# Writing out the order of all five queues in an attention loop, with decays per chunk and four more constant matmuls

## The chip, the cores and the metric

The kernel runs on one core of a Trainium2 chip. The metric is the time on the device in microseconds (us), the median of several executions. The profiled execution has a time of its own, and inside it a span from its first to its last instruction. The engines are PE (TensorE: matrix products into PSUM), DVE (VectorE), ACT (ScalarE), POOL (GpSimd) and SP (SyncE, which here only issues DMAs). Each takes its instructions from one queue, in order.

## The reference, cut to what matters

```python
B, H, S, D = 4, 8, 576, 64
gamma = 1 - 2.0 ** (-5 - arange(H))
Dmat = where(i >= j, gamma[h] ** (i - j), 0)
ret = ((q @ k.T) / sqrt(D) * Dmat) @ v          # retention, no softmax
x = ret.transpose(0, 2, 1, 3).reshape(B * S, H * D)
x = (silu(x @ w_gate) * (x @ w_val)) @ w_out    # 512 -> 1536 -> 512
y = relu(x @ w2_in) ** 2 @ w2_out               # 512 -> 2048 -> 512
```

The weights w_* are int64 words that hold doubles' bits; the kernel turns them into fp32 pairs (a high and a low part) on the chip.

## The kernel before, in words

**Attention.** The loop runs over n = 0 to 17 and handles 16 pairs of heads, each pair 128 partitions wide. The sequence of 576 is cut into four chunks of 128 and one of 64. For pair n, `scores(n, 0..3)` makes q k products within each of the four chunks (PE, tile `s`, into PSUM), and DVE multiplies by the mask of decays to `p_sb` (L439). `scores(n, (4,))` does the same for the last, short chunk; its result is `pl`. `states(n)` makes K V of each of four chunks (tile `kvs`) and sums them up over the chunks into `sb` (ACT copies the first, DVE adds three, L459). Two iterations later `apply(n, False)` and `apply(n, True)` sum q times state and p times v for the four chunks and for the last one, and ACT evicts to `xy` (L488). The bank that `apply(n - 2, True)` writes to is the one in which `scores(n, (4,))` left its result, so it waits until DVE has read that into `pl`. `prep_state` scales k (tile `kv_sb`, L410, on DVE for the first four pairs, then on POOL) and q (tile `qs`, L414, POOL) by decays that belong to absolute positions, for all chunks: `kscale` has a column for each chunk, `qscale` has 448.

**Loads.** `load(n)` issues on SP qk and kv of pair n, 576 KB each, for the first four pairs also mask and qscale. qk has three buffers, kv four.

**Weights.** A unit is 128 x 512 words. It goes through five steps, `pump` by `pump`: step 1 two ACT instructions (L161, L162) on the raw load; step 2 DVE L164; step 3 ACT and DVE split the unit before into its high and low part (L145, L146 `w_lo`), then DVE L168; step 4 L170; step 5 L179. `fill` is 1 from iteration 3 on. There are two raw buffers. In the loop 14 units are converted.

**Early projection.** Iterations 6 to 17 each do twelve matmuls of the first feed-forward layer for its first 512 tokens (`hidden1_early`), alternately for `g` and `v`, on x split into a high (ACT, `xh`) and a low part (DVE, `xl`).

**What sets the order.** A planner orders each engine's instructions from costs that it assumes, and keeps what the data demand. In the loop PE alone is held to the order of the code: `matmul` puts each instruction behind the one before it. DVE, ACT, POOL and SP are as planned. Behind the loop (`chain["on"] = False`) all is planned.

PE's fp32 matmul appears as two rows in the trace. Matmul rows all have line 98, so they are told apart by tile.

Of the kernel before, what the change touches and what calls it, by code (L numbers as in the profile page):

```python
# [18 lines left out]
NP = H // 2  # L19
# [21 lines left out]
WA = 20  # L41
# [14 lines left out]
def retention_moe_kernel(  # L56
# [34 lines left out]
    chain = {"on": False, "last": None}  # L91

    def matmul(*args, **kw):

        with ExitStack() as behind:
            if chain["on"] and chain["last"] is not None:
                behind.enter_context(tc.issue_after(chain["last"]))
            m = nc.tensor.matmul(*args, **kw)  # L98
        if chain["on"]:
            chain["last"] = m.ins  # L100
        return m
# [10 lines left out]
    def prefetch(upto):  # L112

        while loads["next"] <= min(upto, len(order) - 1):
# [13 lines left out]
            nc.sync.dma_start(out=raw, in_=src.rearrange("p (a n) -> p a n", a=2))  # L128
# [13 lines left out]
    def parts_unit(i):  # L142
        wf = w_t.pop(i).bitcast(F32)
        hi, lo = weight_tiles()
        nc.scalar.copy(hi, wf)  # L145
        nc.vector.tensor_tensor(out=lo, in0=wf, in1=f32(hi), op=ALU.subtract)  # L146
        units[order[i]] = (hi, lo)

    def conversion():
        ts = nc.vector.tensor_scalar  # L150
        for i in range(len(order)):
# [9 lines left out]
            nc.scalar.activation(out=low, in_=low16, func=AF.Copy, scale=2.0**-13)  # L161
            nc.scalar.activation(out=wf, in_=high.bitcast(F32), func=AF.Abs)  # L162
# [7 lines left out]
            nc.vector.scalar_tensor_tensor(  # L170
# [7 lines left out]
            for to, lo in adds:  # L178
                nc.vector.tensor_tensor(out=to, in0=to, in1=lo, op=ALU.add)  # L179
# [35 lines left out]
    def split_x(ph, n, cc):  # L215
# [9 lines left out]
        nc.scalar.copy(hi, src)  # L225
        nc.vector.tensor_tensor(out=lo, in0=src, in1=f32(hi), op=ALU.subtract)
        xs[ph, n, cc] = (hi, lo)

    def three(dst, a, b, first, last):
        (ah, al), (bh, bl) = a, b  # L230
        matmul(dst, ah, bh, start=first, stop=False)
        matmul(dst, ah, bl, start=False, stop=False)
        matmul(dst, al, bh, start=False, stop=last)
# [23 lines left out]
    def halves(key, t, early=False):  # L257
# [6 lines left out]
        nc.scalar.copy(hi, t)  # L264
        nc.vector.tensor_tensor(out=lo, in0=t, in1=f32(hi), op=ALU.subtract)  # L265
        hs[key] = (hi, lo)

    def hidden1(n, f, then=None):
# [3 lines left out]
        nc.scalar.activation(out=t, in_=g, func=AF.Sigmoid)  # L272
        yield
        nc.vector.tensor_tensor(out=t, in0=g, in1=t, op=ALU.mult)  # L274
        yield
        nc.vector.tensor_tensor(out=t, in0=vv, in1=t, op=ALU.mult)  # L276
# [5 lines left out]
    def hidden1_early(k):  # L282

        f, what = k // 2, "gv"[k % 2]
        if k == 0:
            for cc in range(CC):
                split_x(1, 0, cc)
        (ps,) = project(1, 0, f, (what, what))
        if what == "g":
            early_t[f] = t = t_p.tile([P, 512], F32, tag="t", name="t")  # L290
            nc.scalar.activation(out=t, in_=ps, func=AF.Sigmoid)
        t = early_t[f]
        nc.vector.tensor_tensor(out=t, in0=ps, in1=t, op=ALU.mult)
        if what == "v":
            halves((1, 0, f), early_t.pop(f), early=True)
        if k == 2 * HALF - 1:
            for cc in range(CC):
                split_x(1, 1, cc)

    def hidden2(n, f):  # L300
# [3 lines left out]
        nc.scalar.activation(out=t, in_=ps, func=AF.Relu)  # L304
        yield
        nc.vector.scalar_tensor_tensor(  # L306
# [10 lines left out]
    def out1(n, f):  # L317
# [14 lines left out]
        for cc, a in enumerate(acc.pop((1, n))):  # L332
# [5 lines left out]
            if n == 0 and f0:  # L338
                nc.vector.tensor_tensor(out=dst, in0=a[:, :m], in1=dst, op=ALU.add)
            elif cc % 2:  # L340
                nc.vector.tensor_copy(dst, a[:, :m])
            else:
                nc.scalar.copy(dst, a[:, :m])
            if n == 0 and f0 == 0:
                nc.sync.dma_start(out=part[:, cc, :], in_=dst)

    def out2(n, f):
# [7 lines left out]
        if f == F2 - 1:  # L355
            for tt, a in enumerate(acc.pop((2, n))):
# [3 lines left out]
                if tt % 2:  # L360
                    nc.vector.tensor_copy(t, a)
                else:
                    nc.scalar.copy(t, a)
                r0 = CHUNKS[2][n][0] + tt * P
                nc.sync.dma_start(out=out[r0:r0 + P, :], in_=t)
# [4 lines left out]
    with ExitStack() as st:  # L370
# [13 lines left out]
        def warm():  # L384

            one = const.tile([P, 256], F32, tag="one", name="one")
            nc.vector.memset(one, 1.0)
            ps = bank("g")
            for _ in range(WARM):
                matmul(ps[:, :256], one[:, :P], one, start=True, stop=True)  # L390

        def load(n):
# [234 lines left out]
```

## Time and profile before

| what | value |
|---|---|
| median of three runs | 953.1 us (951.22, 953.1, 954.19) |
| profiled execution, time | 950.97 us |
| its span | 949.2 us |
| PE busy in the span | 923.5 us (97%) |
| DVE, ACT, POOL busy | 469.0, 328.1, 33.7 us |
| mean granted clock | 0.986 |

The span is 1.77 us shorter than the time of the same execution. A busy share is a mean over stages: the attention loop ends at about 137.7 us, and the two layers fill the rest.

### The profile page before, as it was taken

The page shows a single profiled execution, that of the slowest core. Times are in us where ns is not written, and L with a number is a line of the kernel's source. Part 1 is how long each engine was busy: PE and PEld are TensorE (multiplying, and loading weights), DVE is VectorE, ACT ScalarE, POOL GpSimd, SP SyncE. Part 2 cuts the span into 40 slices and gives each one's busy share as a digit, 9 for nine tenths or more (in the row PEclk, how much of TensorE's full clock was granted, in tenths as well). Part 3 has the DMA queues.
Part 4 walks back from the last instruction along what each step waited for, and adds up shares of the span by engine and source line. Part 5 has one row for each costly group of instructions (what it writes and reads, how often), then busy time and mean ns, then how long its engine had stood idle before and what let it go on. Part 6 is the DMA issues. An engine that isn't in the chain of part 4 may idle for free.

```text
span 949.2 us, 12499 instructions
## 1 busy us (share of the span) xinstructions
PE 923.5 (97%) x5144; PEld 771.5 (81%) x5144; DVE 469.0 (49%) x849; ACT 328.1 (35%) x597; POOL 33.7 (4%) x35
## 2 busy tenths in 40 slices
PE   8499999999999999999999999999999999999998
PEld 6377778788888998888888888888888888888897
DVE  3858667798423332223799888233224222322232
ACT  1443444564312121112566565232223222322232
POOL 2133300000000000000000000000000000000000
PEclk7799999999999999999999999999999999999999
DMA  8756524442100000000244321001001000100010
GB/s 336 248 186 208 197 89 136 137 150 95 60 1 1 2 1 1 1 1 25 69 132 143 122 89 44 1 1 45 1 1 44 1 1 1 45 0 1 1 45 23
DMA packets 22025, 63.60 MB, mean 67 GB/s; under 512 B 2256, under 2 KB 3792, under 8 KB 21968
## 3 DMA queue, kind: packets, MB, share of 16 engines
q1 hardware_dynamic: 21968, 62.81, 19.8%
q8 instruction: 40, 0.66, 0.3%
q14 instruction: 17, 0.14, 0.0%
HBM read 57.03 MB, written 5.77 MB: 66 GB/s over the span
## 4 chain that ended last, share of the span: by engine, by line
PE 81%; DMA 8%; DVE 7%; ACT 2%; issue 1%; SPq 1%; ACTq 0%; DVEq 0%
PE a L98 34%; PE v L98 23%; PE g L98 23%; DMA raw<-in_w 6%; DVE w L170 1%; DVE w L179 1%; DVE w_lo L146 1%; DMA qk_sb<-in_qk 1%; DVE w L164 1%; DMA part<-part_sb 1%; ACT raw L161 1%; DVE p_sb L439 1%; DVE w L168 1%; DVE w_lo L265 0%; ACT w L162 0%
## 5 line engine op out<-in xcount | busy, mean ns | idle before, releaser
L265 DVE TENSOR_TENSOR h_lo<-t,h_hi 128x512 fp32r<-128x512 f32 (+1 forms) x134 | 85.1, 635 | 67.1 <-ACT h_hi L264 66.7
L264 ACT CAST h_hi<-t 128x512 fp32r<-128x512 f32 (+1 forms) x134 | 77.2, 576 | 118.1 <-DVE t L276 64.5
L98 PE MATMUL g<-xh,w_hi 128*128 128x512 f32 (+1 forms) x304 | 114.1, 375 | 0.8 <-ACT xh L225 0.8
L98 PE MATMUL v<-xh,w_hi 128*128 128x512 f32 (+1 forms) x304 | 113.7, 375 | 0.0
L98 PE MATMUL g<-xh,w_lo 128*128 128x512 f32 (+1 forms) x304 | 113.3, 373 | 0.0
L98 PE MATMUL g<-xl,w_hi 128*128 128x512 f32 (+1 forms) x304 | 113.2, 372 | 0.0
L98 PE MATMUL v<-xh,w_lo 128*128 128x512 f32 (+1 forms) x304 | 113.2, 372 | 0.0
L98 PE MATMUL v<-xl,w_hi 128*128 128x512 f32 (+1 forms) x304 | 113.2, 372 | 0.0
L98 PE MATMUL a<-w_lo,h_hi 128*128 128x512 f32 x288 | 112.3, 390 | 0.0
L98 PE MATMUL a<-w_hi,h_hi 128*128 128x512 f32 x288 | 112.2, 390 | 0.0
L98 PE MATMUL a<-w_hi,h_lo 128*128 128x512 f32 x288 | 109.8, 389 | 0.0
L98 PE MATMUL a<-h_lo,w_hi 128*128 128x512 f32 (+1 forms) x216 | 78.9, 366 | 0.0
L98 PE MATMUL a<-h_hi,w_lo 128*128 128x512 f32 (+1 forms) x216 | 78.9, 365 | 0.0
L98 PE MATMUL a<-h_hi,w_hi 128*128 128x512 f32 (+1 forms) x216 | 77.0, 366 | 1.2 <-ACT h_hi L264 1.2
L306 DVE SCALAR_TENSOR_TENSOR t<-g,t 128x512 f32<-128x512 f32 (+1 forms) x40 | 25.5, 637 | 105.5 <-ACT t L304 105.4
L274 DVE TENSOR_TENSOR t<-g,t 128x512 f32<-128x512 f32 (+1 forms) x54 | 34.0, 630 | 85.1 <-ACT t L272 84.8
L306 DVE SCALAR_TENSOR_TENSOR t<-v,t 128x512 f32<-128x512 f32 (+1 forms) x40 | 25.5, 638 | 92.4 <-ACT t L304 92.1
L98 PEld LDWEIGHTS g<-xh,w_hi 128*128 128x128 f32 x304 | 57.2, 188 | 11.5 <-ACT xh L225 1.2
L98 PEld LDWEIGHTS v<-xh,w_hi 128*128 128x128 f32 x304 | 57.3, 188 | 10.3 <-issue 0.2
L98 PEld LDWEIGHTS g<-xh,w_lo 128*128 128x128 f32 x304 | 57.3, 188 | 10.1
L98 PEld LDWEIGHTS v<-xh,w_lo 128*128 128x128 f32 x304 | 57.3, 188 | 10.1
L98 PEld LDWEIGHTS g<-xl,w_hi 128*128 128x128 f32 x304 | 57.3, 188 | 9.8
(88 smaller groups left out, 1486.0 us busy)
## 6 DMA issues: line engine op xcount, KB each, us to landing
raw<-in_w SPq DMA_DIRECT2D x51, 512.0 KB, 3.6
kv_sb<-in_kv SPq DMA_DIRECT2D x16, 576.0 KB, 5.0
xy<-in_w SPq DMA_DIRECT2D x17, 512.0 KB, 3.8
qk_sb<-in_qk SPq DMA_DIRECT2D x15, 576.0 KB, 5.0
out<-o_sb SPq DMA_DIRECT2D x18, 256.0 KB, 2.3
part<-part_sb SPq DMA_DIRECT2D x4, 256.0 KB, 2.8
xy<-part SPq DMA_DIRECT2D x1, 1024.0 KB, 5.3
qs_sb<-in_qscale SPq DMA_DIRECT2D x4, 224.0 KB, 7.4
```

Source lines behind the costliest of these rows:

```text
L98: m = nc.tensor.matmul(*args, **kw)
L146: nc.vector.tensor_tensor(out=lo, in0=wf, in1=f32(hi), op=ALU.subtract)
L161: nc.scalar.activation(out=low, in_=low16, func=AF.Copy, scale=2.0**-13)
L164: ts(out=wf, in0=wf, scalar1=TINY, scalar2=HUGE, op0=ALU.max, op1=ALU.min)
L168: ts(out=w, in0=w, scalar1=3, scalar2=0x3FFFFFFF, op0=ALU.logical_shift_left, op1=ALU.bitwise_and)
L170: nc.vector.scalar_tensor_tensor(out=w, in0=high, scalar=0xC0000000, in1=w, op0=ALU.bitwise_and, op1=ALU.bitwise_or)
L179: nc.vector.tensor_tensor(out=to, in0=to, in1=lo, op=ALU.add)
L264: nc.scalar.copy(hi, t)
L265: nc.vector.tensor_tensor(out=lo, in0=t, in1=f32(hi), op=ALU.subtract)
L274: nc.vector.tensor_tensor(out=t, in0=g, in1=t, op=ALU.mult)
L306: nc.vector.scalar_tensor_tensor(out=t, in0=ps, scalar=0.0, in1=t, op0=ALU.max, op1=ALU.mult)
L439: nc.vector.tensor_tensor(out=pt[:w], in0=ps[:w, :, :nx * w].rearrange("p h (c q) -> p h c q", c=nx), in1=mask_sb[:w, hp, :, None, :w].to_ ...
```

## The change

Every engine gets a chain of its own (`Chained`): within the loop each instruction is put behind the one before it on the same engine. The code's order is then the order of the five queues, so parts of the loop are moved: the load of kv for pair n + 1 comes ahead of that of qk for n + 2, `prep_state(n + 1)` goes to the end of the iteration, `apply(n - 2, True)` behind the early projection, the splits of x for the projection to one in each of the iterations 3 to 6, those for the next 512 tokens behind the loop. The pumps stand at other places: five steps an iteration as before, four in iteration 3.

Decays belong to chunks: k is scaled by one column of `kscale` for all chunks (two ACT multiplies of 128x256), q by 128 columns that repeat (two POOL instructions of 384 and 64 columns), and the sum of states multiplies the state so far by gamma to the 128 (scalar_tensor_tensor). Of `qscale` 161 columns are loaded instead of 448. In the first pair two matmuls on the constant tile stand behind its scores and two behind its K V (`warm(2)`). WA goes from 20 to 21, so 15 units are converted in the loop.

The diff, cut; `nc.tensor`, `nc.vector`, `nc.scalar`, `nc.gpsimd`, `nc.sync` become `pe`, `dve`, `act`, `pool_e`, `sp` everywhere:

```diff
-WA = 20
+WA = 21
...
+    class Chained:
+        def __init__(self, engine):
+            self.engine, self.last = engine, None
+        def __getattr__(self, name):
+            op = getattr(self.engine, name)
+            def traced(*args, **kw):
+                with ExitStack() as behind:
+                    if chain["on"] and self.last is not None:
+                        behind.enter_context(tc.issue_after(self.last))
+                    i = op(*args, **kw)
+                if chain["on"]:
+                    self.last = i.ins
+                return i
+            return traced
+    pe, dve, act, pool_e, sp = map(Chained, (nc.tensor, nc.vector, nc.scalar, nc.gpsimd, nc.sync))
...
     def hidden1_early(k):
         f, what = k // 2, "gv"[k % 2]
-        if k == 0:
-            for cc in range(CC):
-                split_x(1, 0, cc)
...
-        if k == 2 * HALF - 1:
-            for cc in range(CC):
-                split_x(1, 1, cc)
...
+        def load_qk(n):
             b, hp = pairs[n]
             qk_t[n] = qk_p.tile([P, 2, S], F32, tag="qk", name="qk_sb")
+            for at in (slice(0, CUT), slice(CUT, S)) if n == 0 else (slice(0, S),):
+                sp.dma_start(out=qk_t[n][:, :, at], in_=qk[b, hp][:, :, at])
+                if n == 0 and at.start == 0:
+                    sp.dma_start(out=ks_sb, in_=kscale)
+        def load_kv(n):
+            b, hp = pairs[n]
             kv_t[n] = kv_p.tile([P, 2 * NC - 1, P], F32, tag="kv", name="kv_sb")
+            sp.dma_start(out=kv_t[n], in_=kv[b, hp])
             if n < NP:
-                dma(out=mask_sb[:, n], in_=mask[:, n])
-                dma(out=qs_sb[:, n], in_=qscale[:, n])
+                sp.dma_start(out=mask_sb[:, n], in_=mask[:, n])
+                sp.dma_start(out=qs_sb[:, n], in_=qscale[:, n, P:P + qs_sb.shape[-1]])
...
-            kn = kv_t[n][:, NC:, :].rearrange("p t (h d) -> p t h d", h=2)
-            (nc.gpsimd if n >= NP else nc.vector).tensor_tensor(
-                out=kn, in0=kn, in1=ks_sb[:, hp].to_broadcast([P, NC - 1, 2, D]), op=ALU.mult
-            )
+            for h, r in enumerate(rs):
+                kn = kv_t[n][:, NC:, r]
+                act.mul(kn, kn, ks_sb[:, hp, 1, h])
             qs = q_p.tile([P, S - P], F32, tag="qs", name="qs")
-            nc.gpsimd.tensor_tensor(
-                out=qs, in0=qk_t[n][:, 0, P:], in1=qs_sb[:, hp, :], op=ALU.mult
-            )
+            for c, m in ((0, 3 * P), (3 * P, D)):
+                w = min(m, P)
+                pool_e.tensor_tensor(
+                    out=qs[:, c:c + m].rearrange("p (c q) -> p c q", q=w),
+                    in0=qk_t[n][:, 0, P + c:P + c + m].rearrange("p (c q) -> p c q", q=w),
+                    in1=qs_sb[:, hp, None, :w].to_broadcast([P, m // w, w]), op=ALU.mult,
+                )
...
-                nc.vector.tensor_tensor(out=sb[:, c], in0=ps[:, c], in1=sb[:, c - 1], op=ALU.add)
+                dve.scalar_tensor_tensor(
+                    out=sb[:, c], in0=sb[:, c - 1], scalar=qs_sb[:, pairs[n][1], -1:], in1=ps[:, c],
+                    op0=ALU.mult, op1=ALU.add,
+                )
...
-        load(0)
-        load(1)
+        load_qk(0)
+        load_kv(0)
+        load_qk(1)
         prep_state(0)
...
+            if nxt:
+                load_kv(n + 1)
             if n + 2 <= last:
-                load(n + 2)
+                load_qk(n + 2)
             if n == FROM - 3:
                 prefetch(1)
-            if nxt:
-                prep_state(n + 1)
             if new:
                 scores(n, range(NC - 1))
-            pump(fill)
+            if n == 0:
+                warm(2)
+            pump(fill if n == FROM - 3 else 2 * fill)
             if old:
                 apply(n - LAG, False)
             pump(fill)
+            if LAG < n <= LAG + CC:
+                split_x(1, 0, n - LAG - 1)
             if new:
                 scores(n, (NC - 1,))
+            pump(fill)
+            if new:
                 states(n)
+            if n == 0:
+                warm(2)
             pump(fill)
             if FROM <= n < FROM + 2 * HALF:
                 hidden1_early(n - FROM)
-            pump(fill)
             if old:
                 apply(n - LAG, True)
-            pump(fill)
-
+            if nxt:
+                prep_state(n + 1)
+        for cc in range(CC):
+            split_x(1, 1, cc)
     chain["on"] = False
```

## Rows read from the trace of the kernel before

**Rows 1.** The page: granted TensorE clock (tenths of full speed) in 40 slices of the span.

```profile
PEclk7799999999999999999999999999999999999999
```

**Rows 2.** Busy time in three stretches; then PEclk, DMA share, GB/s.

```profile
0.00:10.00 10.00, 6.44 (x44) 4.62 (x44) 2.68 (x6) 1.50 (x2) 1.24 (x8) 0.93 0.71 228
10.00:25.00 15.00, 13.13 (x156) 10.99 (x156) 7.98 (x17) 4.00 (x9) 4.07 (x4) 0.71 1.03 414
...
51.00:137.70 86.70, 83.88 (x941) 65.88 (x937) 60.14 (x118) 35.49 (x78) 22.87 (x19) 1.00 0.51 171
```

**Rows 3.** PE's timeline: start, duration, instructions merged, idle before and its releaser.

```profile
1.19 3.78 PE L98 MATMUL g<-one 128*128 128x256 f32 x8 [1.19 <-DVE one L387]
...
20.82 1.16 PE L98 MATMUL s<-qk_sb 64*128 64x128 f32 x16
...
31.32 0.48 PE L98 MATMUL s<-qs,sb 64*64 64x64 f32 x4 [5.21 <-DVE pl L439]
...
32.14 2.08 PE L98 MATMUL s<-qk_sb 64*128 64x128 f32 x16
...
43.40 0.48 PE L98 MATMUL s<-qs,sb 64*64 64x64 f32 x4 [5.04 <-DVE pl L439]
...
51.00 1.16 PE L98 MATMUL s<-qk_sb 64*128 64x128 f32 x16
...
58.93 1.16 PE L98 MATMUL s<-qk_sb 64*128 64x128 f32 x16
...
66.20 1.16 PE L98 MATMUL s<-qk_sb 64*128 64x128 f32 x16
...
140.07 0.50 PE L98 MATMUL g<-xh,w_hi 128*128 128x512 f32 x1 [0.78 <-ACT xh L225]
```

**Rows 4.** Timelines of DVE (31 to 33 us) and of POOL (at 32 us).

```profile
30.99 0.28 DVE L439 TENSOR_TENSOR pl<-s,mask_sb 64x128 f32<-64x128 f32 x1
...
31.96 1.41 DVE L168 TENSOR_SCALAR w<-w 128x512 uint32<-128x512 uint32 x1
...
31.95 1.14 POOL L414 TENSOR_TENSOR qs<-qk_sb,qs_sb 128x448 f32<-128x448 f32 x1 [3.06 <-issue]
```

**Rows 5.** The chain that ended last, first 60 us: start, length, what.

```profile
14.43 7.89 DMA raw<-in_w
...
52.76 1.90 PE o L98 x28
...
55.53 2.94 PE g L98 x12
```

**Rows 6.** Tile kv_sb, to 130 us: its loads.

```profile
DMA to landing us min/median/max: 3.6/5.0/8.4
```

**Rows 7.** Groups of instructions by shape, to 160 us: busy us, mean ns, idle before.

```profile
L439 DVE TENSOR_TENSOR p_sb<-s,mask_sb 128x1024 f32<-128x1024 f32 x16 | 19.4, 1215 | 0.5 <-PE s L98 0.3
...
L170 DVE SCALAR_TENSOR_TENSOR w<-raw,w 128x512 uint32<-128x512 uint32 x19 | 14.6, 767 | 0.1
L179 DVE CUSTOM_DVE_ANT_0 w<-raw,w 128x1024 uint16<-128x1024 uint16 x19 | 14.5, 765 | 0.1
...
L146 DVE TENSOR_TENSOR w_lo<-w,w_hi 128x512 fp32r<-128x512 f32 x19 | 13.1, 690 | 1.4 <-ACT w_hi L145 1.4
...
L459 DVE TENSOR_TENSOR sb<-kvs,sb 128x64 f32<-128x64 f32 x48 | 10.5, 218 | 10.2 <-ACT sb L457 9.6
...
L168 DVE TENSOR_SCALAR w<-w 128x512 uint32<-128x512 uint32 x20 | 9.3, 467 | 0.2
L488 ACT COPY xy<-o 128x512 f32<-128x512 f32 x16 | 9.2, 576 | 9.7 <-PE o L98 9.6
...
L226 DVE TENSOR_TENSOR xl<-xy,xh 128x512 fp32r<-128x512 f32 x8 | 6.1, 770 | 6.3 <-ACT xh L225 6.2
...
L488 ACT COPY xy<-s 128x64 f32<-128x64 f32 x16 | 3.3, 209 | 3.3 <-PE s L98 3.3
```

**Rows 8.** Line 164, to 51 us: duration min/median/max, first and last start.

```profile
L164 DVE TENSOR_SCALAR w<-w x6: 414/422/430, 23.6 to 43.3; 128x512 f32<-128x512 f32 x6
```

More of the change, by code (lines that the diff above doesn't have):

```diff
@@ L89, in f32 @@
         return ap.bitcast(F32)
[L91 to L101, printed above, removed]
+    chain = {"on": False}
+    class Chained:
[13 more added lines that the diff above has]
+    pe, dve, act, pool_e, sp = map(Chained, (nc.tensor, nc.vector, nc.scalar, nc.gpsimd, nc.sync))
     units = {}
@@ L160, in conversion @@
             wf = w.bitcast(F32)
-            nc.scalar.activation(out=low, in_=low16, func=AF.Copy, scale=2.0**-13)
-            nc.scalar.activation(out=wf, in_=high.bitcast(F32), func=AF.Abs)
+            act.activation(out=low, in_=low16, func=AF.Copy, scale=2.0**-13)
+            act.activation(out=wf, in_=high.bitcast(F32), func=AF.Abs)
             yield
@@ L178, in conversion @@
             for to, lo in adds:
-                nc.vector.tensor_tensor(out=to, in0=to, in1=lo, op=ALU.add)
+                dve.tensor_tensor(out=to, in0=to, in1=lo, op=ALU.add)
             del raw_t[i]
@@ L224, in split_x @@
             lo = xs_p.tile([P, N], F32R, tag="xl", name="xl")[:, :m]
[L225 to L226 removed]
+        act.copy(hi, src)
+        dve.tensor_tensor(out=lo, in0=src, in1=f32(hi), op=ALU.subtract)
         xs[ph, n, cc] = (hi, lo)
@@ L230, in three @@
         (ah, al), (bh, bl) = a, b
-        matmul(dst, ah, bh, start=first, stop=False)
-        matmul(dst, ah, bl, start=False, stop=False)
-        matmul(dst, al, bh, start=False, stop=last)
+        pe.matmul(dst, ah, bh, start=first, stop=False)
+        pe.matmul(dst, ah, bl, start=False, stop=False)
+        pe.matmul(dst, al, bh, start=False, stop=last)
     def cut(pair, a, n):
@@ L263, in halves @@
             lo = h_p.tile([P, N], F32R, tag="hl", name="h_lo")[:, :m]
-        nc.scalar.copy(hi, t)
-        nc.vector.tensor_tensor(out=lo, in0=t, in1=f32(hi), op=ALU.subtract)
+        act.copy(hi, t)
+        dve.tensor_tensor(out=lo, in0=t, in1=f32(hi), op=ALU.subtract)
         hs[key] = (hi, lo)
@@ L338, in out1 @@
             if n == 0 and f0:
-                nc.vector.tensor_tensor(out=dst, in0=a[:, :m], in1=dst, op=ALU.add)
+                dve.tensor_tensor(out=dst, in0=a[:, :m], in1=dst, op=ALU.add)
             elif cc % 2:
-                nc.vector.tensor_copy(dst, a[:, :m])
+                dve.tensor_copy(dst, a[:, :m])
             else:
-                nc.scalar.copy(dst, a[:, :m])
+                act.copy(dst, a[:, :m])
             if n == 0 and f0 == 0:
-                nc.sync.dma_start(out=part[:, cc, :], in_=dst)
+                sp.dma_start(out=part[:, cc, :], in_=dst)
     def out2(n, f):
@@ L382, in retention_moe_kernel, with warm @@
         pairs = [(b, hp) for b in range(B) for hp in range(NP)]
-        def warm():
-            one = const.tile([P, 256], F32, tag="one", name="one")
-            nc.vector.memset(one, 1.0)
+        def warm(k):
             ps = bank("g")
-            for _ in range(WARM):
-                matmul(ps[:, :256], one[:, :P], one, start=True, stop=True)
-        def load(n):
+            for _ in range(k):
+                pe.matmul(ps[:, :256], one[:, :P], one, start=True, stop=True)
+        def load_qk(n):
```

61 lines of the change are left out of this document (28 added, 33 removed).

## The prediction, made before the changed kernel was run

> **What bounds the kernel now.** I read the page first, for the clock by slice [rows 1], then the stretches [rows 2], then TensorE's (PE's) timeline of the first 140 us [rows 3], because only code up to the end of the attention loop is changed. What can be won lies in the first 137.7 us, where the loop's last product ends. The reader is to see three things there.
>
> First, from 51.00 us on, an iteration with its early projection costs 7.27 us (58.93 to 66.20), and the stretch 51.0 to 137.7 has 2.82 us of PE idle in 86.70 [rows 2, 3]. That stretch is nearly full.
>
> Second, ahead of 51.0 it is not. The scores of iteration 3 start at 20.82 us, those of iteration 4 at 32.14, those of iteration 6 at 51.00: ten us each, where an attention pair without projection needs 7.27 - 2.94 = 4.33 (2.94 is a projection of twelve matmuls) [rows 3, 5]. PE stood still 5.21 us, and later 5.04 us (43.40), until the vector engine (DVE) had written `pl` [rows 3]. DVE did so at 30.99 [rows 4]; it was busy with conversions, of which the planner put six ahead of 43.7 us [rows 8].
>
> Third, idle time costs twice: the granted clock is 0.7 in the first two slices [rows 1], and sixteen score instructions take 2.08 us at 32.14 (1.2 GHz, after the 5.21 us of standing still) against 1.16 at 58.93 (2.4 GHz) [rows 3].
>
> **The change part by part.**
>
> *The chains* add no instruction. They fix the order on DVE, ScalarE (ACT), GpSimd (POOL) and SP as written. What matters is where `pl` of iteration n now stands on DVE, and that `apply(n-2, True)`, whose bank is that of `pl`, has moved behind the projection. From iteration 4 on DVE does after the scores: p_sb, step 5 of one conversion (L179), step 2 of the next (L164), in iterations 3 to 6 one `xl`, then `pl`. The rest (w_lo, L168, three state sums, L170, the hidden product) comes behind it.
>
> *K scaled on ACT.* DVE loses 4 x 0.692 us, POOL 12 of its larger instructions; ACT gains two copies of 128x256 with a scale per partition for each pair. No row has that form. 64 columns cost 209 ns and 512 cost 576 [rows 7], so 256 should cost 209 + 367 x 192/448 = 366, 0.73 us a pair; bounds 0.42 and 1.15 (two at either row). ACT was busy 35.49 of 86.70 us [rows 2], so it has room. But ACT is now in order: the copies wait for kv(n+1), and behind them stand the conversion's two ACT steps, the eviction to xy, and so `xl` and `pl`. kv lands 3.6 to 8.4 us after its issue, median 5.0 [rows 6]; it is issued as iteration n starts and wanted as it ends, 7.27 us later in the steady part. I take no wait there.
>
> By the row, ACT pays 0.73 us a pair. The Trainium skill, "ScalarE: Activation LUTs", section "What ACT_TABLE_LOAD costs", gives 186 ns + 0.833 ns a column and about 93 ns more for each pointer operand: 492 ns here, 0.98 us a pair. That speaks against the move, by 0.25 us in each of iterations 3 to 5 where ACT can hold DVE, 0.75 in the sum at most. No row here shows the form.
>
> *q scaled on POOL* in two pieces of 384 and 64 columns: between one and two of the present instruction (1.14 us, [rows 4]), on an engine busy 22.87 of 86.70 us [rows 2]. Nothing. It does free DVE a little: an L168 that overlaps a POOL instruction took 1.41 us where its mean is 0.467 [rows 4, 7], and POOL now has half as much to do. The Trainium skill, "GPSIMD Engine Reference", section "Key points", says that POOL shares its memory interfaces with DVE, with contention where DVE has two SBUF inputs or a two-port mode. This row agrees. If every such overlap went, 0.9 us an iteration would; I count none of it, since the walk below uses means.
>
> *State sums* become scalar_tensor_tensor: 218 ns now; at 512 columns that form has 767 against 690 for tensor_tensor [rows 7], so at most 0.024 more each, 0.07 a pair. Nothing.
>
> *Loads.* qscale shrinks from 448 to 161 columns, 224 to 80.5 KB, four times: 0.59 MB, 1.4 us at the 414 GB/s of the saturated stretch [rows 2]. kv(n+1) and qk(n+2) come in another order, and the first weights now come behind kv(4) and qk(5) on SP, whose kv(4) waits for `apply(0, True)`. Before they were issued at 14.43 and the first landed at 22.32 [rows 5].
>
> *Four warm matmuls*: eight rows; eight such rows took 3.78 us at the start [rows 3], so 1.9 us for each group at that price, half as much at the full clock. The first 10 us have 3.56 us of idle PE [rows 2] in waits for qk and kv, so they lie mostly inside; up to 0.5 each may stick out, ahead of scores that wait for qk(1) anyhow. What they may give is a clock that stays up through iterations 1 and 2. I take nothing: that stretch waits for loads (1.03 DMA share, [rows 2]), and iteration 3 for its weights.
>
> *One more weight unit* (15 for 14) inside the loop: 3.2 us of DVE moved (0.47 for L164, as L168, and four rows of [rows 7]), from a part where PE does not wait for it.
>
> **The walk.** Bytes up to the first weight unit, by the code: six qk and five kv of 576 KB, masks 512, qscale 322, kscale 16, one unit 512: 7,698 KB = 7.88 MB. 2.28 are in by 10 us [rows 2]; 5.60 at 414 GB/s take 13.5: 23.5 us. With a gap while kv(4) waits, and the latency, I take 25.0. Bounds: 23.5, and 27.1 if kv(4) is only issued at 20.8 (where iteration 3 starts now), 3.6 to land, and 1.11 MB more behind it.
>
> Iteration 3 (PE gets there by 19 or 20, and stops ahead of `apply(1, True)`): two ACT steps of 128x512, 1.3 (each a little over the eviction's 0.576), eviction 0.58, xh as much, xl 0.77, pl 0.28: 28.5. The product 0.7 to 0.8: iteration 4 starts at 29.2 (32.14 now).
>
> Iteration 4, low clock: scores 2.08, to 31.3. p_sb on DVE meanwhile; the apply takes 1.90 at the high clock [rows 5] and up to 1.8 times that at the low one, I take 2.6, to 33.9; eviction, xh, xl, pl: 0.58 + 0.6 + 0.77 + 0.28, to 36.1. Product 0.6: iteration 5 at 36.7.
>
> Iteration 5, clock up again. DVE behind pl at 36.1: w_lo 0.69, L168 0.47, sums 0.65, L170 0.77 to 38.7 (the means of [rows 7]); p_sb 1.2, L179 0.77, L164 0.47, xl 0.77, pl 0.28 to 42.2. Product 0.5: iteration 6 at **42.7**, against 51.00: **-8.3 us**. Bounds 40 (weights at 23.5, and 1.2 less where the steps overlap or the clock holds) and 46 (weights at 27.1, a POOL overlap in 4 and in 5).
>
> *Iterations 6 to 17.* `pl` is ready 1.2 + 0.77 + 0.47 + 0.28 = 2.7 us after the scores (3.5 with an xl); PE wants it after apply, two small groups and the projection, 5.9 us. So the wait for `pl` goes, which was part of the 2.82 idle. I take half back: **-1.4**, bounds -2.8 and +2 (0.4 us in each iteration with a `v`, where the product waits for the projection and its split for ACT's cast).
>
> *The end of the loop.* The splits of the second chunk now come after the last eviction: 0.21 + 0.6 + 0.77 = 1.6 us ahead of PE's second matmul, where it now stands 0.78 at 140.07 [rows 3]: **+0.8**, bounds -0.8 and +1.6. PE's later order is still planned, and may cover it.
>
> Sum: -8.3 - 1.4 + 0.8 = **-8.9 us**. The profiled execution is 950.97 (span 949.2 and 1.77 around it): 942.1. It lies 2.13 under the median of the runs, 953.1, so the forecast for a median is **944.2 us**. All bounds together: -14.6 and -1.4, that is 938.5 to 951.7.
>
> **The rivals.** *Late weights.* Everything on ACT and DVE in iteration 3 now stands behind one load. Each us later is a us lost: at 27.1, 2.1 us, so 946.3; with a low clock in iteration 5 as well (0.9 for its scores, about as much for its apply) 948.2. For it: that load landed 7.89 us after its issue in a full queue [rows 5], and PE must stand still some six us whatever happens, so the clock falls. Against: 1.4 us of qscale less ahead of it. Chance 0.20.
>
> *Little change.* The order as written could make iterations 4 and 5 as long as now, pl waiting each time for eviction, xh and xl in a row at the low clock (about 9 us each rather than 7.5 and 6), with the late weights on top: iteration 6 then starts at 29.2 + 2.1 + 18 = 49.3, and -1.7 - 1.4 + 0.8 = -2.3 gives 950.8. Against: the five-us holds came with conversions bunched ahead of pl [rows 8], and two steps of one, L179 and L164, stand there now. Chance 0.14.
>
> *DVE becomes the bound (slower).* By 51.0 us DVE had begun six of 14 units [rows 8]; now it does under three of 15 by iteration 6, so some four more units of 3.2 us fall into the twelve iterations, and 60.1 us [rows 2] becomes 73 in about 84. In a fixed order it also waits. Two iterations need 2 x 5.3 + three hidden instructions of 0.7 + 0.7 of waiting for the cast = 13.4 us, against PE's 14.5. From 16.0 it eats the gain (6 x 1.5 us); at 17.0 it costs 15 us, 959. For that it needs 3.6 us more in every two iterations, four overlaps like the one of [rows 4]. Chance 0.08; in between it ends near 953.
>
> **How the numbers follow.** Forecast 0.58, late weights 0.20, little change 0.14, slower 0.08. A measurement here tells 0.3%, 2.9 us, from no change. The first two are faster (0.78); little change is mostly the same (0.13); slower 0.09 with a bit of it. The range must leave out no more than 0.2: 939 to 950.5 holds the forecast and most of the late weights.
>
> **What would show it.** In the profile after: iteration 4's scores near 29, iteration 6's near 42.7 and the last products near 127.5; one wait of about six us of PE for pl, not two; the first weights landing near 25; no wait of ACT for kv over 1 us from iteration 6 on; DVE under 90% busy there. Wrong if PE waits for pl or for state sums in the steady part, if ACT sits behind kv each time, or if the first layer's plan shifts.

## The result and the profile after

The changed kernel takes **944.2 us** (median of four, 943.19 to 944.67) against 953.4 for the kernel before in the same session: ratio 0.9906, 95% interval 0.9887 to 0.9924. The forecast was 944.2, in a range of 939.0 to 950.5. Its profiled execution took 944.21 us, with a span of 942.4.

That the two figures meet is partly luck, and the profile shows it. Before, the profiled execution (950.97) lay 2 us under its own median, and the forecast carried that distance over; after, the profiled execution lies on its median. So the forecast for the profiled execution was 942.1, and it took 944.2. Each of the three terms of the sum was off by some 1.8 us, two of them one way and one the other.

All instructions in the loop now pass through one helper and have one line, L106; they are told apart by tile. First the slices of the page, to be read against [rows 1]:

```profile
PE 921.7 (98%) x5152; PEld 769.7 (82%) x5152; DVE 466.0 (49%) x845; ACT 340.8 (36%) x629; POOL 21.0 (2%) x39
...
PEclk9899999999999999999999999999999999999999
```

One slice is under 0.9, where two stood at 0.7. The stretches, against [rows 2]:

```profile
0.00:10.00 10.00, 6.71 (x38) 4.76 (x40) 1.68 (x3) 2.19 (x3) 1.97 (x9) 1.00 0.72 239
10.00:25.00 15.00, 13.26 (x190) 10.69 (x190) 6.67 (x14) 4.05 (x11) 3.52 (x6) 0.89 0.94 352
25.00:42.00 17.00, 10.00 (x128) 8.27 (x128) 10.33 (x21) 8.43 (x20) 3.02 (x4) 0.80 0.55 188
42.00:130.00 88.00, 84.92 (x965) 66.97 (x962) 70.45 (x141) 50.27 (x112) 12.50 (x20) 1.00 0.59 199
```

(Columns: stretch and length, busy us of PE, weight loads, DVE, ACT, POOL, then granted clock, DMA share, GB/s.) Then PE's timeline, to be read against [rows 3], with the score instructions `s<-qk_sb 64*128` as the start of each iteration:

```profile
19.50 1.16 PE L106 MATMUL s<-qk_sb 64*128 64x128 f32 x16
...
30.66 0.48 PE L106 MATMUL s<-qs,sb 64*64 64x64 f32 x4 [7.30 <-DVE pl L106]
...
31.48 2.08 PE L106 MATMUL s<-qk_sb 64*128 64x128 f32 x16
...
38.34 0.33 PE L106 MATMUL s<-qs,sb 64*64 64x64 f32 x4 [1.34 <-DVE pl L106]
...
38.87 1.16 PE L106 MATMUL s<-qk_sb 64*128 64x128 f32 x16
...
44.07 0.33 PE L106 MATMUL s<-qs,sb 64*64 64x64 f32 x4 [1.34 <-DVE pl L106]
...
44.59 1.16 PE L106 MATMUL s<-qk_sb 64*128 64x128 f32 x16
...
127.65 0.34 PE L106 MATMUL s<-pl,kv_sb 128*64 128x64 f32 x4
129.73 0.50 PE L106 MATMUL a<-w_hi 128*128 128x512 f32 x1 [1.75 <-ACT xy L106]
...
130.80 0.63 PE L106 MATMUL a<-w_lo,w_hi 128*128 128x512 f32 x1
...
134.18 0.40 PE L106 MATMUL a<-w_hi 128*128 128x512 f32 x1
```

Iterations 3, 4, 5, 6 start at 19.50, 31.48, 38.87, 44.59 where it was 20.82, 32.14, 44.21 and 51.00: **-6.4 us** by iteration 6. Of it 4.7 lie between iterations 4 and 5 (7.39 us instead of 12.07), 1.3 in the earlier start of iteration 3 and 1.1 between iterations 5 and 6; iteration 3 itself takes 0.7 us longer. The start of iteration 5 before, which [rows 3] does not show:

```profile
44.21 2.08 PE L98 MATMUL s<-qk_sb 64*128 64x128 f32 x16
```

The two holds of five us have become one of 7.30 and two of 1.34, and in sum they are hardly shorter (9.98 for 10.25 us). With two small waits ahead of `kvs` gone as well, PE's idle time from iteration 3 to iteration 6 falls from 12.1 to 10.0 us. The rest is the clock: PE is busy for 15.1 us of that stretch instead of 18.1 with as many matmuls, at a granted clock of 0.86 instead of 0.77, and the scores of iteration 5 take 1.16 us where they took 2.08. From 44.6 to 127.9 PE shows no idle time at all, and the last product of the loop starts at 127.65: that stretch takes 83.4 us instead of 86.7, **-3.3**. At the end PE stands still 1.75 us, 0.97 longer than before, and after it eight matmuls go at a pitch of 0.42 us where the later ones have 0.23 (some 1.5 us), **+2.5** in all. The three make -7.2; the last matmul ends 7.3 us earlier.

The wait at the end has its cause on ACT. The first product behind the loop waits for the last eviction, and that stands behind three instructions of the weight conversion, the first of which had waited 2.20 us for its load:

```profile
127.84 0.67 ACT L106 ACTIVATE raw<-raw 128x512 uint32<-128x512 uint16 x1 [2.20 <-DMA raw<-in_w]
128.41 0.65 ACT L106 ACTIVATE w<-raw 128x512 f32<-128x512 f32 x1
128.96 0.61 ACT L106 CAST w_hi<-t 128x512 fp32r<-128x512 f32 x1
129.47 0.21 ACT L106 COPY xy<-s 128x64 f32<-128x64 f32 x1
```

The splits of x that now come behind the loop hold nothing: the first product that needs one starts at 136.03 us, without a wait.

Why PE is held for 7.30 us, on ACT, DVE and SP's queue:

```profile
19.73 0.91 ACT L106 ACTIVATE kv_sb<-kv_sb,ks_sb 128x256 f32<-128x256 f32 x2
27.41 0.65 ACT L106 ACTIVATE raw<-raw 128x512 uint32<-128x512 uint16 x1 [6.78 <-DMA raw<-in_w]
27.97 0.64 ACT L106 ACTIVATE w<-raw 128x512 f32<-128x512 f32 x1
28.52 0.57 ACT L106 COPY xy<-o 128x512 f32<-128x512 f32 x1
28.98 0.62 ACT L106 CAST xh<-xy 128x512 fp32r<-128x512 f32 x1
```

```profile
28.64 0.43 DVE L106 TENSOR_SCALAR w<-w 128x512 f32<-128x512 f32 x1 [6.71 <-ACT w L106]
29.63 0.69 DVE L106 TENSOR_TENSOR xl<-xy,xh 128x512 fp32r<-128x512 f32 x1 [0.56 <-ACT xh L106]
30.24 0.28 DVE L106 TENSOR_TENSOR pl<-s,mask_sb 64x128 f32<-64x128 f32 x1
```

```profile
19.65 0.33 SPq L106 DMA_DIRECT2D kv_sb<-in_kv  x1
20.07 0.38 SPq L106 DMA_DIRECT2D qk_sb<-in_qk  x1
20.50 1.08 SPq L106 DMA_DIRECT2D raw<-in_w  x2
```

The eviction and `pl` need nothing of the weights, but stand behind instructions that do. Whoever reads only "PE waits for DVE pl" sees a slow DVE; DVE had waited 6.71 us itself.

### The profile page after: what moved, and what is told of

It is laid out like the page before. It is cut to its first block, busy times and chain, and to the rows that moved or that the text cites. A ratio compares the mean times of both kernels' runs of the same rounds, so it can differ in the third digit from the quotient of the medians.

```text
span 942.4 us, 12541 instructions
## 1 busy us (share of the span) xinstructions
PE 921.7 (98%) x5152; PEld 769.7 (82%) x5152; DVE 466.0 (49%) x845; ACT 340.8 (36%) x629; POOL 21.0 (2%) x39
## 4 chain that ended last, share of the span: by engine, by line
PE 80%; DMA 9%; DVE 6%; ACT 3%; issue 1%; SPq 0%; ACTq 0%
PE a L106 31%; PE g L106 22%; PE v L106 21%; DMA raw<-in_w 6%; DVE w L106 3%; PE s L106 3%; PE o L106 3%; DMA xy<-in_w 2%; DVE w_lo L106 1%; ACT raw L106 1%; PE kvs L106 1%; ACT w L106 1%; DVE t L106 1%; DMA kv_sb<-in_kv 1%; ACT xy L106 0%
## 5 line engine op out<-in xcount | busy, mean ns | idle before, releaser
L106 ACT ACTIVATE t<-g 128x512 f32<-128x512 f32 (+1 forms) x100 | 55.4, 554 | 211.0 <-PE g L106 210.8
L106 ACT CAST h_hi<-t 128x512 fp32r<-128x512 f32 (+1 forms) x134 | 77.0, 575 | 120.1 <-DVE t L106 114.5
L106 DVE TENSOR_TENSOR h_lo<-t,h_hi 128x512 fp32r<-128x512 f32 (+1 forms) x134 | 85.2, 636 | 69.7 <-ACT h_hi L106 69.3
L106 PE MATMUL g<-xh,w_hi 128*128 128x512 f32 (+1 forms) x304 | 113.9, 375 | 0.0
L106 PE MATMUL v<-xh,w_hi 128*128 128x512 f32 (+1 forms) x304 | 113.8, 374 | 0.0
L106 PE MATMUL g<-xh,w_lo 128*128 128x512 f32 (+1 forms) x304 | 113.3, 373 | 0.0
L106 PE MATMUL v<-xh,w_lo 128*128 128x512 f32 (+1 forms) x304 | 113.2, 373 | 0.0
L106 PE MATMUL g<-xl,w_hi 128*128 128x512 f32 (+1 forms) x304 | 113.2, 372 | 0.0
L106 PE MATMUL v<-xl,w_hi 128*128 128x512 f32 (+1 forms) x304 | 113.2, 372 | 0.0
L106 PE MATMUL a<-w_lo,h_hi 128*128 128x512 f32 x288 | 112.3, 390 | 0.0
L106 PE MATMUL a<-w_hi,h_hi 128*128 128x512 f32 x288 | 112.2, 390 | 0.0
L106 PE MATMUL a<-w_hi,h_lo 128*128 128x512 f32 x288 | 110.1, 389 | 0.0
L106 DVE TENSOR_TENSOR t<-g,t 128x512 f32<-128x512 f32 (+1 forms) x60 | 38.1, 636 | 89.4 <-ACT t L106 89.2
L106 PE MATMUL a<-h_lo,w_hi 128*128 128x512 f32 (+1 forms) x216 | 79.0, 366 | 0.2 <-DVE h_lo L106 0.2
L106 PE MATMUL a<-h_hi,w_lo 128*128 128x512 f32 (+1 forms) x216 | 78.9, 366 | 0.0
L106 DVE SCALAR_TENSOR_TENSOR t<-g,t 128x512 f32<-128x512 f32 (+1 forms) x40 | 25.5, 639 | 105.5 <-ACT t L106 105.4
L106 PE MATMUL a<-h_hi,w_hi 128*128 128x512 f32 (+1 forms) x216 | 76.6, 366 | 0.8 <-ACT h_hi L106 0.8
L106 DVE TENSOR_SCALAR w<-w 128x512 f32<-128x512 f32 (+1 forms) x136 | 57.4, 423 | 26.9 <-ACT w L106 25.4
L106 DVE SCALAR_TENSOR_TENSOR t<-v,t 128x512 f32<-128x512 f32 (+1 forms) x40 | 25.6, 639 | 90.0 <-ACT t L106 89.7
L106 PEld LDWEIGHTS g<-xh,w_hi 128*128 128x128 f32 x304 | 57.3, 188 | 10.4 <-issue 0.2
L106 PEld LDWEIGHTS v<-xh,w_hi 128*128 128x128 f32 x304 | 57.3, 188 | 10.3 <-issue 0.2
L106 PEld LDWEIGHTS v<-xh,w_lo 128*128 128x128 f32 x304 | 57.3, 188 | 10.0
```

What stands on the lines that cost most here:

```text
L106: i = op(*args, **kw)
```

## The experiments

All are timed against the kernel before, whose median was about 952 us in the sessions of the experiments and 953.4 in that of the changed kernel. The expectations were written before each ran. The starts are read from the one profiled execution of each kernel. It lay 2.4 us under the median with old decays (941.85), 1.3 under it with PE chained alone (944.16) and with the old order (945.24), and within one us elsewhere.

| run | us | ratio, 95% interval | iterations 4 / 6 start |
|---|---|---|---|
| changed kernel | 944.2 | 0.9906 (0.9887 to 0.9924) | 31.48 / 44.59 |
| without the warm matmuls | 944.1 | 0.9919 (0.9905 to 0.9933) | 30.14 / 43.18 |
| old decays | 944.3 | 0.9912 (0.9898 to 0.9927) | 31.33 / 44.45 |
| PE chained alone | 945.5 | 0.9933 (0.9915 to 0.9950) | 24.42 / 35.67 |
| old order, chains alone | 946.5 | 0.9935 (0.9914 to 0.9956) | 28.07 / 39.82 |
| last splits inside | 944.1 | 0.9915 (0.9902 to 0.9928) | 31.29 / 44.33 |
| raw loads in iteration 2 | 941.4 | 0.9884 (0.9866 to 0.9902) | 27.34 / 40.13 |
| conversion from iteration 4 | 936.4 | 0.9826 (0.9807 to 0.9845) | 24.28 / 35.96 |
| both | 936.5 | 0.9836 (0.9822 to 0.9849) | 24.41 / 35.87 |
| both, splits inside, early table | 935.9 | 0.9829 (0.9814 to 0.9844) | 23.97 / 36.99 |
| both, `pl` ahead of `xl` | 934.2 | 0.9805 (0.9789 to 0.9821) | 23.07 / 35.69 |
| all of it | 934.2 | 0.9807 (0.9790 to 0.9823) | 22.74 / 34.74 |

**Without the warm matmuls.**

```diff
-            if n == 0:
-                warm(2)
```

(at both places).

> The changed kernel without the four extra matmuls in the first pair. Theory (order): the gain comes from where pl and apply stand on the queues; the extra matmuls only keep PE's clock up in iterations 1 and 2, and what they give is what iteration 3 comes earlier: 20.82 us before, 19.50 after. Without them the granted clock from 10 to 25 us falls from 0.89 to about 0.7, iteration 3 starts 0.5 to 1.5 us later, kv(4), issued behind apply(0, True), and the first weights behind it as well: 944.7 to 945.7 us. Rival (clock): a PE that stays at 2.4 GHz is most of the gain; then at least half of the 9 us is lost, 949 or more.

944.1 us, the same. The clock in the stretch 10 to 25 us is 0.90 with them gone and 0.89 with them there, and iteration 3 starts at 18.77, 0.7 earlier. So the theory had their effect on the clock wrong, and the rival's 949 did not come either. They are neither the gain nor a cost.

**Old decays** (K by DVE and POOL with the old scale, q in one instruction, plain sums of states, 14 units in the loop; the chains and the order as changed).

```diff
-            for h, r in enumerate(rs):
-                kn = kv_t[n][:, NC:, r]
-                act.mul(kn, kn, ks_sb[:, hp, 1, h])
+            (pool_e if n >= NP else dve).tensor_tensor(
+                out=kn, in0=kn, in1=ks_sb[:, hp].to_broadcast([P, NC - 1, 2, D]), op=ALU.mult
+            )
```

> The changed kernel with the old decays: a kscale column for each chunk, k scaled on DVE and POOL, q in one POOL instruction, plain sums, the whole qscale loaded, WA 20; order and chains as changed. Theory (order): 1.4 us of loads come back ahead of the first weights, k scaled by POOL costs DVE an overlap in iterations 4 and 5 (0.9 each), but ACT is freed of 0.91 us a pair and of the table load behind kv(0) (1.28 us): 944 to 947. Rival (fewer bytes and a free POOL are the gain): 949 or more.

944.3 us, inside the theory's 944 to 947. The decays move work between engines and change nothing in the time. One reading is still worth showing, DVE's lines by form from 53 to 128 us: with the old decays, then in the changed kernel (count, busy us, mean ns).

```profile
L106 DVE TENSOR_TENSOR w_lo<-w,w_hi 128x512 fp32r<-128x512 f32 x10 | 12.1, 1208 | 4.3 <-ACT w_hi L106 4.3
...
L106 DVE SCALAR_TENSOR_TENSOR w<-raw,w 128x512 uint32<-128x512 uint32 x12 | 8.2, 684 | 0.1
```

```profile
L106 DVE TENSOR_TENSOR w_lo<-w,w_hi 128x512 fp32r<-128x512 f32 x11 | 7.6, 693 | 5.0 <-ACT w_hi L106 5.0
L106 DVE SCALAR_TENSOR_TENSOR sb<-sb,qs_sb,kvs 128x64 f32<-128x64 f32 x27 | 7.5, 279 | 0.6
L106 DVE SCALAR_TENSOR_TENSOR w<-raw,w 128x512 uint32<-128x512 uint32 x11 | 7.5, 685 | 0.1
```

With K on POOL, `w_lo` takes 1208 ns instead of 693, while the weight steps stay at 684: in a written order the same instruction meets POOL's multiply of K as long as there is a K to scale (eight of the ten; the two behind the last K take 0.69 us). POOL's starts at 64.38, 71.66, 79.02, DVE's `w_lo` at 64.62, 71.87, 79.24 us, for instance. Before, in the planned order, L170 and L179 carried it (878 and 876 ns). The change takes 10 x 0.515 = 5.2 us off DVE, and PE, which shows no wait in that stretch with either decays, is none the faster.

**PE chained alone** (the code as changed, the other four queues planned).

```diff
-    pe, dve, act, pool_e, sp = map(Chained, (nc.tensor, nc.vector, nc.scalar, nc.gpsimd, nc.sync))
+    pe = Chained(nc.tensor)
+    dve, act, pool_e, sp = nc.vector, nc.scalar, nc.gpsimd, nc.sync
```

> The changed kernel in all its parts, with the chain on PE alone; DVE, ACT, POOL and SP are planned again. Theory (order): the planner puts conversions ahead of pl as before; PE again stands still some five us twice ahead of iteration 6, though apply behind the projection helps from there on: 948 to 952 us, iteration 6 at 48 to 51 us. Rival (the moved lines and the decays are enough, chains on the four other queues do nothing): within 1 us of 944.2, iteration 6 at 44 to 46.

945.5 us: the time is 1.3 from the changed kernel's, just outside the rival's one us, by a path that neither foresaw. The planner put the raw loads at 14.11 us, PE's holds for `pl` ahead of iteration 6 are 1.47 and 0.16 us, and iteration 6 starts at 35.67, nine us *ahead* of the changed kernel and 15 ahead of the kernel before. It gives back the nine: from iteration 6 to the end of the loop it takes 92.5 us instead of 83.4, and PE is idle for 8.2 of them. Its waits between 60 and 118 us (us in total, times, longest):

```profile
PE kvs L106 <- DVE sb L468: 2.4, 4, 1.5
PE s L106 <- ACT xy L500: 1.7, 2, 0.9
PE s L106 <- DVE pl L448: 1.2, 3, 0.6
```

With the lines moved, the written order of the other four queues is worth nine us in the steady part and costs nine ahead of it. (Against the kernel before, which took 86.7 us for the steady part, the changed kernel is 3.3 better there.) That shows where a better version lies.

**Old order, chains alone** (the kernel before, with chains on PE, DVE, ACT and POOL in the order of its own code; SP stays planned, since in that order its queue would block itself: kv(5) waits for a buffer that is freed by work behind later loads).

```diff
+    pe, dve, act, pool_e = map(Chained, (nc.tensor, nc.vector, nc.scalar, nc.gpsimd))
+    sp = nc.sync
```

> The kernel before with chains on PE, DVE, ACT and POOL in the order of its own code (SP stays planned; in that code's order it could not stand), nothing else changed: decays, splits, places of prep_state and pumps as before. Theory (lines and chains need one another): in the old order the four splits of the first chunk stand in a row in iteration 6 ahead of the projection (about 3 us of PE), k is scaled at the head of an iteration with p_sb behind it, so the chains alone give little: 948 to 954 us. Rival (the chains alone are the gain, the moved lines are not): 943 to 946.

946.5 us, some two thirds of the gain: between theory and rival. The planner, which still orders SP, put the raw loads at 14.38 us, and iteration 6 starts at 39.82. Ahead of the first projection four splits stand in a row, and PE waits there 1.41 and 3.05 us:

```profile
45.10 0.51 PE L106 MATMUL g<-xh,w_hi 128*128 128x512 f32 x1 [1.41 <-ACT xh L106]
...
48.65 0.70 PE L106 MATMUL g<-xl,w_hi 128*128 128x512 f32 x1 [3.05 <-DVE xl L106]
...
53.49 1.16 PE L106 MATMUL s<-qk_sb 64*128 64x128 f32 x16
```

From 53.49 on six iterations take 7.27 us each (the seventh starts at 97.09). So the steady gain is there with the chains on DVE, ACT and POOL, with decays and code order as before. Iteration 6 takes 13.67 us, 6.4 more than the next ones, 4.5 of them in these two waits: that is the most that the moved splits can buy.

**Last splits inside the projection.**

```diff
         (ps,) = project(1, 0, f, (what, what))
+        if k == 2 * HALF - 1:
+            for cc in range(CC):
+                split_x(1, 1, cc)
```

(and gone from behind the loop).

> The changed kernel with the four splits of the second chunk behind the last projection, ahead of its hidden product, instead of behind the loop. Theory (the end of the loop costs twice): PE stands still 1.75 us after the last product, and its clock then falls for eight matmuls of 0.43 instead of 0.23 us, 1.6 us; with x split by then, the projections of the second chunk follow at once, and 2 to 3.3 us are won: 941 to 942.5 us. Rival (the planner's order behind the loop starts with products whose bank waits for the last eviction whatever is split): 944.

The wait of 1.75 us at the end becomes 0.37 and the low clock behind it is gone. Together that should be worth 2.9 us. Yet the time is 944.1, as the rival said, though not for its reason: the first products behind the loop are now projections, and they wait for nothing. In the profiled execution iteration 6 ran in part at a low clock, and iteration 7 starts at 53.17, 1.3 us later than in the changed kernel (51.88). And from the loop's last product to the end of the span it takes 813.3 us instead of 814.4, so only 1.1 of the 2.9 are kept there: PE waits 0.68 us (at 183.54) and 0.73 (at 217.97) for `h_lo`, where the changed kernel shows one such wait of 0.19. The place of the loss at the end of the loop is shown; what it is worth is not.

**Raw loads in iteration 2, conversion from iteration 4, and both.** Two edits, in a table of two by two with the changed kernel.

```diff
-            if n == FROM - 3:
+            if n == FROM - 4:
                 prefetch(1)
```

```diff
-WA = 21
+WA = 20
...
-            fill = PUMPS[0] if n >= FROM - 3 else 0
+            fill = PUMPS[0] if n >= FROM - 2 else 0
...
-            pump(fill if n == FROM - 3 else 2 * fill)
+            pump(fill if n == FROM - 2 else 2 * fill)
```

> The changed kernel with the first two weight loads issued one iteration earlier, ahead of kv(4) and qk(5). Theory: the 7.30 us that PE stands still in iteration 3 is the landing of the first weights at 27.4 us, which waits through SP's order for apply(0, True) at 19.6. Issued near 15, they land near 20 to 21, the hold shrinks to 1 to 2 us, PE's clock stays up, iteration 4 starts near 25 instead of 31.5 and iteration 6 near 38: 937 to 939 us. Rival (DVE's or ACT's work ahead of pl sets the hold, or kv(4) and qk(5), now behind the weights, hold iteration 4 instead): 942 to 945.

> The changed kernel with the first weights loaded in iteration 2 and converted from iteration 4 on instead of 3 (14 units in the loop, WA 20). Theory: what holds iteration 3 is the first conversion, of which pl needs nothing; without it the hold falls from 4.07 us (weights loaded early) or 7.30 to about 1, PE's clock stays at 2.4 GHz, iteration 4 starts near 24 and iteration 6 near 35: 935 to 938 us. Rival (DVE or the one more unit left for behind the loop takes it back): 941 or more, as with the early loads alone.

> The changed kernel with its raw loads where they are (issued in iteration 3), but with conversion put into the chains from iteration 4 and not from iteration 3. Theory (start of conversion and arrival of the first weights are both needed): the raw weights land at about 27.4 us as in the changed kernel, iteration 4 starts near 24.4 and is held for about 3 us on pl behind the conversion's wait for them, iteration 6 at about 39, 938 to 941 us. Rival (the place of the conversion alone is the gain, the loads' time is covered): no hold over 1.5 us, iteration 6 at about 36, 936 to 937 us.

Loads early alone: 941.4; the raw weights land at 23.39 instead of 27.41 and the hold shrinks from 7.30 to 4.07, 3.2 us, of which the time kept 2.8. That lies between theory and rival: issued at 15.22, the weights land some three us later than the theory had them. Both: 936.5, as expected. Conversion later alone: 936.4, where the theory said 938 to 941, so the rival holds: once conversion begins in iteration 4, the place of the loads is worth nothing. The loads land at 26.41 there, ACT waits 1.00 us for them and the hold of iteration 4 is 1.56 us, two tenths more than its neighbours:

```profile
23.75 0.33 PE L106 MATMUL s<-qs,sb 64*64 64x64 f32 x4 [1.34 <-DVE pl L106]
...
24.28 1.16 PE L106 MATMUL s<-qk_sb 64*128 64x128 f32 x16
...
29.70 0.33 PE L106 MATMUL s<-qs,sb 64*64 64x64 f32 x4 [1.56 <-DVE pl L106]
...
30.23 1.16 PE L106 MATMUL s<-qk_sb 64*128 64x128 f32 x16
```

The theory took the whole time from the start of iteration 4 to the landing for a hold. But ACT comes to its first conversion step only at 25.41, when it has scaled the next pair's k, and a wait of 1.00 us there adds only two tenths to the hold. With no 7.30 us of standing still the scores of iteration 4 also take 1.16 us and not 2.08. The old decays above had 14 units in the loop as well and gained nothing, so the missing unit is not the cause. One choice in the written order, the iteration in which conversion starts, costs **7.8 us** in the changed kernel.

**Both, with the splits inside and an early table load** (a small ACT copy ahead of the first load's wait).

```diff
+        act.copy(q_p.tile([P, S - P], F32, tag="qs", name="qs")[:, :8], one[:, :8])
         warm(WARM)
```

> The kernel of the run before (weights loaded in iteration 2, converted from iteration 4 on), and with it the splits of the second chunk behind the last projection, and a copy of eight columns on ACT at the start, so that ACT's table load comes ahead of the wait for kv(0). Theory: the three add up, 1 us at the start where iterations 0 to 2 don't wait for loads, 2 to 3.3 at the end: 931 to 935 us. Rival (the table load is hidden in the wait for qk(1) and kv(1), the end as after): 0 to 1 us less than the run before.

935.9: 0.6 us less, as the rival said, and no more than the two intervals leave open. The wait at the end falls to 0.40, and iteration 4 has its scores at a low clock (1.80 us).

**`pl` ahead of `xl`**, on both, and on everything.

```diff
-            if LAG < n <= LAG + CC:
-                split_x(1, 0, n - LAG - 1)
             if new:
                 scores(n, (NC - 1,))
+            if LAG < n <= LAG + CC:
+                split_x(1, 0, n - LAG - 1)
```

> The changed kernel with raw loads in iteration 2 and conversion from iteration 4, and besides the split of the first hidden chunk's transposed operand (xh, xl) put behind the scores on the new chunk, so that the product pl stands ahead of xl in VectorE's chain. Theory (the 1.34 us holds that are left in iterations 3 to 5 come from VectorE's chain, which goes through the eviction, xh and xl before the product pl that TensorE waits for): the three holds go, 3 x 1.34 = 4.0 us; iteration 4 at about 23, iteration 6 at about 31.9, 931.5 to 933.5 us. Rival (TensorE then waits at the application for xl, or the stretch is bound by something else): a wait of about 1 us turns up elsewhere in the same iterations, 935 us or more, within 1.5 us of the kernel without this move (936.5).

> The same move in the kernel that also has the last splits inside the projection and the early table load. Theory: again about 4 us, 930 to 933 us, iteration 4 at about 22.5 and iteration 6 near 31. Rival: a wait elsewhere or a low clock after the holds takes it back, 934.5 us or more.

934.2 us with either: 2.3 and 1.7 less than without, where the theory said four and the rival at most 1.5: between the two. The hold of iteration 3 is gone (iteration 4 at 23.07). Those of iterations 4 and 5 stay, since there the conversion stands ahead of `pl`:

```profile
27.15 1.08 PE L106 MATMUL kvs<-kv_sb 128*64 128x64 f32 x16 [0.83 <-ACT kv_sb L106]
29.41 0.33 PE L106 MATMUL s<-qs,sb 64*64 64x64 f32 x4 [1.18 <-DVE pl L106]
...
35.17 0.33 PE L106 MATMUL s<-qs,sb 64*64 64x64 f32 x4 [1.36 <-DVE pl L106]
```

```profile
28.65 0.43 DVE L106 TENSOR_SCALAR w<-w 128x512 f32<-128x512 f32 x1 [3.14 <-ACT w L106]
28.99 0.28 DVE L106 TENSOR_TENSOR pl<-s,mask_sb 64x128 f32<-64x128 f32 x1
```

So the theory on `xl` was right for one hold of three, and what that one gave was soon lost: without the splits inside, iteration 4 starts 1.34 us earlier than in the kernel with both edits (24.41), but PE then waits 0.83 us ahead of `kvs` for ACT's scaling of k, which itself had waited 3.19 us for the load of kv; `kvs` takes 1.08 us where 0.69 is usual; and at iteration 6 0.2 us are left (35.69 against 35.87). Where its 2.3 us come from, the two profiles do not show. A kernel at 934.2 beats the changed one by ten us, with no new instruction, one weight unit less in the loop, and its lines in another order.

## Why the prediction came out right, and where it was wrong

- **What bounds: right. The mechanism: right in part.** The gain lies ahead of iteration 6 and in small waits behind it; PE does no less work. That it does not come from the decays or the warm matmuls is shown: without them the time is 944.3 and 944.1. That it is the chains which bring iteration 6 forward, as the walk has it, is not. With the moved lines and PE chained alone iteration 6 starts at 35.67, with chains on all but SP in the old order at 39.82, with everything at 44.59, against 51.00 before. Each half gives some two thirds of the whole gain by itself. What the chains are shown to give is the steady part: 83.4 us in the changed kernel and 7.27 an iteration in the old order, against 92.5 with the moved lines and PE alone chained.
- **"Iteration 6 at 42.7, -8.3": mis-sized, -6.4.** The weights landed at 27.4, not 25.0. They were issued at 20.50, behind kv(4) at 19.65 and qk(5), as the walk's late bound assumed (27.1). So iteration 4 began at 31.48, in that rival's place. Its price of one us for each us of delay held there (2.4 later; 2.3 later at iteration 4). Part came back, because the scores were followed by 7.39 and 5.72 us, against 7.5 and 6.0 in the walk. What the prediction named "late weights" is what happened early in the loop. That rival had the path right and gave 946.3; the time is not there only because the steady part gave 1.9 us more than forecast.
- **"One wait of about six us for `pl`, not two": half right.** It is one of 7.30, and two of 1.34 that the walk had in its sum but did not name.
- **"-1.4 for iterations 6 to 17": mis-sized, -3.3.** The whole 2.82 us of idle went, not half; for the other half us no view names a cause. The wait named was also wrong: the waits view of the kernel before between 51 and 137.7 us puts 1.8 us of the idle time to ACT's eviction `xy`, and only 0.3 to `pl`.

```profile
PE s L98 <- ACT xy L488: 1.2, 1, 1.2
PE o L98 <- ACT xy L488: 0.6, 1, 0.6
PE kvs L98 <- issue: 0.6, 2, 0.3
PE s L98 <- DVE pl L439: 0.3, 1, 0.3
```

- **"`apply(n - 2, True)` has moved behind the projection": an error of reading.** In the code before it already stood there, and the list of moved parts in the description of the change has it wrong as well; the pumps, splits and `prep_state` around it moved. Nothing in the sum was priced by it, but it was given as a reason, and it is none.
- **"+0.8 at the end": mis-sized, +2.5.** The wait grew by 0.97, near the term, but not by its cause: the splits are covered, and PE waits for the last eviction, which stands behind the conversion on ACT. What the term left out is the clock behind the wait: eight matmuls from 130.80 to 134.18, 3.38 us where 8 x 0.23 = 1.84 would do. That is not sure to come back: in the kernel without the warm matmuls 1.60 us of the same wait are followed by the full clock.
- **The profiled execution's distance to the median** (2.13 us) was carried into the forecast and did not recur. It makes up for the sum of the three errors, +1.9 - 1.9 + 1.7. The last products start at 127.65 where 127.5 was forecast, because the first two of these cancel: luck as well.
- **K on ACT: 0.91 us a pair, not 0.73.** The Trainium skill, "ScalarE: Activation LUTs", section "What ACT_TABLE_LOAD costs", would make it, as an estimate, 0.98, or 0.89 with the overlap of about 93 ns that it gives for two in a row; the measured pair agrees with the latter. It costs no time here: the kernel with old decays took as long.
- **State sums: 279 ns, not 218 to 242.** 0.18 us a pair, hidden, as the rest of DVE is.
- **"DVE becomes the bound": did not come.** DVE is busy 58.98 of 75 us between 53 and 128, 79%, and PE waits for nothing. ACT shows no wait for kv from iteration 6 on, as forecast.
- **Warm matmuls: nothing, right.**

What stays open: the worth of the wait at the end of the loop (above), which single chain of DVE, ACT and POOL removes the steady waits, and whether the changed kernel with only SP left to the planner would have its weights in time. The chains were not tried one by one, and SP was not left out of them alone.

## What to carry to other kernels

A written order on in-order queues makes every instruction behind a late load late, whether it needs that load or not: `pl`, for which PE's next product waited, stood on DVE behind a conversion step and an `xl`, and both of these waited for ACT, where the conversion waited for late weights. It cost 7.8 us until conversion began one iteration later. Use the chains where the loop is full, and walk each queue at the start of the loop, asking of every instruction what it stands in front of. When two kernels have equal times, compare the start of each iteration as well: with PE chained alone it was nine us ahead at iteration 6 and nine behind afterwards, and the better version took the good half of each.

## What was not expected of the hardware

In the changed kernel ACT's table load started only when the load of kv had landed, for which the instruction behind it waits, and so its 1.28 us came between that load and K's scaling:

```profile
7.62 1.28 ACT L106 ACT_TABLE_LOAD   x1 [7.62 <-DMA kv_sb<-in_kv]
8.91 0.91 ACT L106 ACTIVATE kv_sb<-kv_sb,ks_sb 128x256 f32<-128x256 f32 x2
```

It need not: in the kernel before it ran at 0.74 us, though ACT's first instruction there waited for PE until 9.27, and with the early copy at 0.74 as well, which brought K's scaling to 7.52. Why it waits in the one case and not in the other is not shown.

And the clock does not fall at the same place in each kernel. The changed kernel keeps the full clock in iteration 6 after its two holds of 1.34 us (scores 1.16). The kernels with no warm matmuls, with the loads early and with the last splits inside have the same two holds, and the scores of iteration 6 take 1.53, 1.80 and 1.56 us there. At the end of the loop 1.75 us of standing still is followed by the low level, about 1.1 us after PE has resumed; with conversion from iteration 4, holds of 1.34, 1.56 and 1.34 us and one of 1.69 at the end of the loop are followed by none. In the three kernels named an iteration 6 of 8.8 us stands for the 7.29 of the changed kernel, 1.6 us, as much as several of the differences measured here; a difference of that size is not explained by one profile.
